# Strided attention heads on four 64x64 quadrants of the PE array

## The chip, the cores and the metric

The kernel runs on one core of a Trainium2 chip, as one launch. Its time is the device time of that launch in microseconds (us); the kernel before took 598.16 us in the median of three runs (596.69 to 599.0). A core has five engines with their own instruction streams: PE (the matrix array; the profile shows its weight loads apart, as PEld), DVE (vector), ACT (scalar), POOL and SP. Here SP issues nearly all input transfers, in order.

## The reference

Two parts follow each other. The first is attention over 8 batches and 8 heads of 576 positions and 64 features, in float32. Heads 0 to 3 see the 32 latest positions (local). Heads 4 to 7 see the positions of the same residue modulo 32 that are not later (strided):

```python
scores = scale * np.matmul(q, k.transpose(0, 1, 3, 2))
mask_local = (rel >= 0) & (rel < stride)
mask_strided = (rel >= 0) & (pos[None, :] % stride == pos[:, None] % stride)
...
attn = np.exp(scores)
attn = attn / (np.sum(attn, axis=-1, keepdims=True) + 1e-09)
return np.matmul(attn, v).astype(np.float32)
```

For a strided head this is 32 separate problems, one for each residue, of 18 queries by 18 keys. The second part is a mixture of experts: each of the 4608 rows of 512 numbers goes to the best of 8 experts (512 to 1024 to 512, relu) and is weighted by its gate.

## The kernel before

The attention is cut into 32 units: 16 local ones (two batches, one head) and 16 strided ones (`Strided`, one batch, two heads), which take turns. The order of PE's instructions is written out by hand in the loop over `n`: scores of unit `n`, transposes (`turn`) of unit `n-2`, masks of unit `n+1`, values of unit `n-3`, and then pieces of the routing of finished batch pairs (`xl`, `lg`, `xs`, `lt`, `rk`, `en` in the rows). The orders on DVE, ACT and POOL come from a scheduler at build time, which places instructions by its own estimates. Transfers on SP are held back behind named PE instructions (`behind`), three units ahead for q and k. PSUM is one pool of eight banks; a bank is used again when its last reader is done. After the attention the expert part runs from some 165 us to the end; the change leaves its code alone.

A strided unit does this. `prep` copies q into a block-diagonal buffer `qz` (L408: one head on DVE, the other on ACT), with zeros between, so that one product over 128 rows gives the scores of both heads for one residue. `masks` writes the causal mask into one PSUM bank by a bf16 product (L412). `scores` adds 32 products of 36 weight columns and 18 moving columns (L419). A float32 product is two instructions with weights of their own, so the trace counts 64. Softmax runs over 288 columns: L431, L433, L436, L437, L438, L440 on DVE, and L434 (exponential) on ACT. `turn` makes four transposes (L218, tile `ts`) and spreads them into `eb`, with zeros between residues: half by DVE (L450), half by ACT (L454, twice). `values` makes 16 products over 72 rows (four residues of 18 keys), 64 weight columns, 72 moving columns (L464), and ACT copies both banks out (L472). In both products the output rows 0 to 63 and 64 to 127 belong to two column halves of the array, and each product uses the array's full height.

Of the kernel before, what the change touches and what calls it, by code (L numbers as in the profile page):

```python
# [11 lines left out]
F32 = mybir.dt.float32  # L12
# [34 lines left out]
BIG = -float(2 ** 30)  # L47
# [4 lines left out]
C_RE8 = C_ID + P  # L52
C_SIO = C_RE8 + E
C_P = C_SIO + NBP * LA
C_T = C_P + 1
C_F = C_T + 4
C_H = C_F + 4
C_N = C_H + 2

# [6 lines left out]
M_ID = 0  # L66
M_L = M_ID + P
M_S = M_L + 9 * 64
M_TRI = M_S + 16 * 18
M_ONE = M_TRI + P  # L70
M_N = M_ONE + P

# [6 lines left out]
def _block(i, bb):  # L79

    return (i + 2 * bb) % 18


def _constants():
# [7 lines left out]
    for t in range(4):  # L92
        cf[18 * t:18 * t + 18, C_T + t] = 1
# [12 lines left out]
    a = np.arange(18)  # L106
    causal = np.where(a[None, :] <= a[:, None], 0, BIG)
    for j in range(2):
        for h in range(2):
            r0 = 64 * j + 18 * h  # L110
            cb[r0:r0 + 18, M_S:M_S + 288] = np.tile(causal, (1, 16))
    cb[:, M_TRI:M_TRI + P] = -(np.arange(P)[:, None] >= np.arange(P)[None, :]).astype(np.float32)
    cb[:, M_ONE:M_ONE + P] = 1
    tok = P * np.arange(36)[None, :] + np.arange(P)[:, None]
    return cf, cb.astype(ml_dtypes.bfloat16), tok.astype(np.float32)


def _layout(q, k, v, moe_modality_id, moe_w_gate, moe_modality_bias, moe_w1, moe_w2):
    q, k, v = (np.asarray(t, np.float32) for t in (q, k, v))
# [7 lines left out]
    vr = v[:, :4].reshape(NBP, 2, 4, 18, 32, D).transpose(0, 2, 1, 3, 4, 5)  # L127
# [3 lines left out]
    for bb in range(2):  # L131
        for i in range(18):
# [3 lines left out]
            w = win[:, :, i % 2, :, 2 * (i // 2) + bb] if i < 16 else win[:, :, i - 16, :, 16 + bb]  # L136
# [11 lines left out]
    vs = v[:, 4:].reshape(B, 2, 2, 18, 4, 2, 4, D).transpose(0, 1, 6, 3, 4, 5, 2, 7)  # L148
    vs = np.ascontiguousarray(vs).reshape(B, 2, 72, 1024)
# [10 lines left out]
    cf, cb, tok = _constants()  # L160
# [22 lines left out]
def attention_moe(ctx: ExitStack, tc: tile.TileContext, a, out):  # L183
    nc = tc.nc
# [6 lines left out]
    def pa(name):  # L191
        return ps.tile([P, 512], F32, tag="a", name=name)
# [38 lines left out]
    pin = tc.keep_in_program_order  # L231
# [8 lines left out]
    def behind(dma, last):  # L240
        return pin(follow(dma, last))
# [45 lines left out]
    qzs = zeros(2, [P, 32, 2, 18], "qz")  # L287
    for t in qds + ets:
        nc.vector.memset(t[:], 0.0)
    for t in qzs:  # L290
        nc.gpsimd.memset(t[:], 0.0)


    class Local:
# [92 lines left out]
    class Strided:  # L387
# [9 lines left out]

        def load_values(self, part, last):
            if part == 0:
                self.vs = lp.tile([72, 8, 2, D], F32, tag="vs", name=f"vs{self.n}")  # L400
                behind(nc.sync.dma_start(self.vs.rearrange("p g h d -> p (g h d)"), a["vs"][self.b, self.pr]), last)
# [8 lines left out]
        def masks(self):  # L410
            self.s = pa(f"ss{self.n}")[:, :288]
            nc.tensor.matmul(self.s, identb, cb[:, M_S:M_S + 288], start=True, stop=True)  # L412

        def scores(self):
            n, qz, s = self.n, self.qz, self.s
            for i in range(16):
                for j in range(2):
                    r = (i // 4) * 8 + j * 4 + i % 4
                    at["scores"] = nc.tensor.matmul(  # L419
                        s[64 * j:64 * j + 36, 18 * i:18 * i + 18],  # L420
                        qz[:, r, :, :].rearrange("p h q -> p (h q)"),
                        self.qk[:, 1, 18 * r:18 * r + 18],
                        start=False, stop=True, skip_group_check=True,
                    )
            s3 = s.rearrange("p (i k) -> p i k", i=16)

            def bc(t):
                return t.unsqueeze(2).to_broadcast([P, 16, 18])

            mx = lp.tile([P, 16], F32, tag="mxs", name=f"mxs{n}")  # L430
            nc.vector.tensor_reduce(mx[:], s3, AX.X, ALU.max)  # L431
            ex = lp.tile([P, 16, 18], F32, tag="exs", name=f"exs{n}")
            nc.vector.tensor_tensor(ex[:], s3, bc(mx), ALU.subtract)  # L433
            nc.scalar.activation(ex[:], ex[:], AF.Exp, scale=0.125)  # L434
            sm = lp.tile([P, 16], F32, tag="sms", name=f"sms{n}")
# [3 lines left out]
            self.en = lp.tile([P, 16, 18], F32, tag="ens", name=f"ens{n}")  # L439
            nc.vector.tensor_tensor(self.en[:], ex[:], bc(sm), ALU.mult)  # L440

        def turn(self):
            n = self.n
            tp = pa(f"ts{n}").rearrange("p (g q) -> p g q", g=4)
            for g in range(4):
                turned_to(tp[0:72, g, :], self.en[:, 4 * g:4 * g + 4, :])
            self.eb = eb = lp.tile([72, 8, 4, 36], F32, tag="eb", name=f"eb{n}")
            src = tp[0:72].rearrange("p g (j x) -> p (g j) x", j=2)[:, :, 0:36]
            sh = [72, 8, 2, 36]
            nc.vector.tensor_tensor(  # L450
                eb[:, :, 0:2, :], src.unsqueeze(2).to_broadcast(sh),
                cf[0:72, C_T:C_T + 2].unsqueeze(1).unsqueeze(3).to_broadcast(sh), ALU.mult)
            for t in (2, 3):
                nc.scalar.activation(eb[:, :, t, :], src, AF.Copy, scale=cf[0:72, C_T + t:C_T + t + 1])  # L454

        def values(self):
            n, eb, vs, b = self.n, self.eb, self.vs, self.b
            for g2 in range(2):
                ot = pa(f"ot{n}{g2}")[:, :288]
                for g in (2 * g2, 2 * g2 + 1):  # L460
                    for j in range(2):
                        c = (g % 2) * 144 + 72 * j
                        for h in range(2):
                            at["values"] = nc.tensor.matmul(  # L464
                                ot[64 * h:64 * h + 64, c:c + 72],
                                vs[:, 2 * g + j, h, :],
                                eb[:, 2 * g + j, :, 18 * h:18 * h + 18],
                                start=True, stop=True, skip_group_check=True,
                            )
                base = (b % 2) * S  # L470
                dst = self.xc[:, base:base + S].rearrange("p (q r) -> p r q", r=32)[:, 16 * g2:16 * g2 + 16, :]
                nc.scalar.copy(dst, ot.rearrange("p (r q) -> p r q", r=16))  # L472

    rows = []

# [515 lines left out]
    for ph, (bp, n) in enumerate(PHASES):  # L991
        last = ph == len(PHASES) - 1
# [154 lines left out]
```

## Time and profile before

| | us |
|---|---|
| median of 3 runs | 598.16 |
| lowest, highest | 596.69, 599.0 |
| the profiled execution, whole | 600.58 |
| its span (first to last instruction) | 598.8 |
| mean granted clock of PE in it | 0.986 of full |

The profiled execution is 2.42 us above the median. Its span lacks 1.78 us that lie around it. Busy times overlap where instructions are pipelined, so a sum of durations is larger than the time that they take; the chain of waits gives the steps without that overlap. A row of the trace is one instruction or several alike (`x64`). `issue` is time in which an engine waits for nothing that the profile shows.

### The profile page before, as it was taken

How to read it: one execution, taken by the hardware profiler on the slowest of the kernel's cores; microseconds unless marked ns; L12 is line 12 of the kernel's file. 1: busy time of each engine (PE TensorE's matmuls, PEld its weight loads, DVE VectorE, ACT ScalarE, POOL GpSimd, SP SyncE). 2: the span in 40 equal slices, each digit the busy share in tenths (PEclk: the TensorE clock that was granted, in tenths of full speed). 3: DMA queues.
4: the chain of work that ended last, by engine and by line, in shares of the span. 5: the costliest groups of instructions: out<-in, count | busy, mean ns of one | idle time of the engine just before them, and what ended most of it. 6: DMA issues, size and time to landing. Idle time of an engine off the chain costs nothing.

```text
span 598.8 us, 15262 instructions
## 1 busy us (share of the span) xinstructions
PE 574.2 (96%) x5995; PEld 508.0 (85%) x5997; DVE 439.1 (73%) x1092; ACT 395.0 (66%) x814; POOL 249.0 (42%) x226
## 2 busy tenths in 40 slices
PE   8998889897999999999999999999999999999995
PEld 5887778776879898999999989999999999999995
DVE  6885967954868799668687687687687787787542
ACT  5897868764785676676566576665665665665652
POOL 1021101126247636554544746546545646532311
PEclk9999989988899999999999999999999999999998
DMA  8997978987745843744843844213214239514631
GB/s 316 301 295 218 346 242 282 318 293 248 253 108 159 235 146 97 235 156 103 243 153 98 221 168 92 71 37 106 71 36 106 71 113 278 110 45 71 221 103 50
DMA packets 72482, 102.03 MB, mean 170 GB/s; under 512 B 48019, under 2 KB 48275, under 8 KB 68820
## 3 DMA queue, kind: packets, MB, share of 16 engines
q0 software_dynamic: 20672, 58.01, 29.1%
q1 hardware_dynamic: 51252, 42.48, 26.7%
q8 instruction: 49, 0.80, 0.6%
q10 hardware_dynamic: 480, 0.51, 0.3%
q14 instruction: 29, 0.24, 0.1%
HBM read 123.45 MB, written 19.18 MB: 238 GB/s over the span
## 4 chain that ended last, share of the span: by engine, by line
PE 85%; DVE 4%; issue 4%; DMA 3%; ACT 2%; POOL 0%; SPq 0%; POOLq 0%; ACTq 0%; DVEq 0%
PE h L921 34%; PE o L935 33%; PE o L369 3%; PE ot L464 2%; DMA vs<-in_vs 2%; PE s L334 2%; PE ss L419 2%; PE xs L218 1%; PE lg L524 1%; PE t L218 1%; PE ts L218 1%; PE xl L218 1%; DMA qks<-in_qks 1%; PE en L620 1%; ACT wh L956 1%
## 5 line engine op out<-in xcount | busy, mean ns | idle before, releaser
L957 DVE TENSOR_TENSOR wl<-raw,wh 128x512 fp32r<-128x512 f32 x288 | 187.8, 692 | 66.0 <-ACT wh L956 52.5
L956 ACT CAST wh<-raw 128x512 fp32r<-128x512 f32 x288 | 163.9, 619 | 71.5 <-PE o L935 49.5
L921 PE MATMUL h<-xh,wl 128*128 128x256 f32 x576 | 162.7, 283 | 0.0
L921 PE MATMUL h<-xl,wh 128*128 128x256 f32 x576 | 162.6, 283 | 0.0
L921 PE MATMUL h<-xh,wh 128*128 128x256 f32 x576 | 162.4, 282 | 0.2 <-ACT wh L956 0.2
L803 POOL DMA_INDIRECT raw<-in_w,wi x72 | 92.6, 1286 | 158.1 <-DVE wl L957 121.4
L921 PEld LDWEIGHTS h<-xh,wh 128*128 128x128 f32 x576 | 109.5, 190 | 7.6 <-issue 0.6
L921 PEld LDWEIGHTS h<-xl,wh 128*128 128x128 f32 x576 | 109.6, 190 | 5.5
L935 PE MATMUL o<-wh,hh 128*128 128x512 f32 x288 | 114.3, 397 | 0.0
L935 PE MATMUL o<-wl,hh 128*128 128x512 f32 x288 | 113.8, 395 | 0.0
L921 PEld LDWEIGHTS h<-xh,wl 128*128 128x128 f32 x576 | 109.7, 190 | 1.0
L935 PE MATMUL o<-wh,hl 128*128 128x512 f32 x288 | 110.3, 390 | 0.0
L924 ACT ACTIVATE hh<-h 128x256 fp32r<-128x256 f32 x144 | 55.4, 384 | 67.2 <-PE h L921 50.1
L926 DVE SCALAR_TENSOR_TENSOR hl<-h,hh 128x256 fp32r<-128x256 f32 x144 | 60.7, 421 | 30.7 <-ACT hh L924 23.4
L935 PEld LDWEIGHTS o<-wh,hl 128*128 128x128 f32 x288 | 53.5, 188 | 11.0
L935 PEld LDWEIGHTS o<-wh,hh 128*128 128x128 f32 x288 | 54.6, 189 | 7.8 <-ACT hh L924 0.2
L935 PEld LDWEIGHTS o<-wl,hh 128*128 128x128 f32 x288 | 54.6, 190 | 5.6
L943 POOL DMA_INDIRECT out<-y,le x36 | 44.2, 1229 | 20.7 <-ACT y L942 11.0
L794 POOL DMA_INDIRECT le<-ld,li x36 | 39.6, 1101 | 12.9 <-issue 10.1
L787 POOL DMA_INDIRECT fx<-xd,le x36 | 40.1, 1115 | 11.0 <-issue 10.7
L479 POOL DMA_DIRECT2D xd<-xt x20 | 14.5, 725 | 61.9 <-ACT xt L488 61.9
L369 PEld LDWEIGHTS o<-vv,et 128*64 128x64 f32 x512 | 21.2, 156 | 10.1 <-issue 7.6
(192 smaller groups left out, 779.8 us busy)
## 6 DMA issues: line engine op xcount, KB each, us to landing
vv<-in_vl SPq DMA_DIRECT2D x32, 292.5 KB
qks<-in_qks SPq DMA_DIRECT2D x32, 288.0 KB
xd<-xt POOLq DMA_DIRECT2D x16, 512.0 KB
qk<-in_qkl SPq DMA_DIRECT2D x16, 304.0 KB
qk<-in_qkl SPq DMA_DIRECT2D x16, 288.0 KB
vs<-in_vs SPq DMA_DIRECT2D x16, 288.0 KB
raw<-in_w,wi POOLq DMA_INDIRECT x72
xd<-xt POOLq DMA_DIRECT2D x4, 256.0 KB
```

Source lines behind the costliest of these rows:

```text
L218: at["turn"] = nc.tensor.transpose(dst, src, ident)
L369: at["values"] = nc.tensor.matmul(o[64 * jj:64 * jj + 64, k, :], et[:, u, :, :].rearrange("p g q -> p (g q)"), vv[:, u, :], start=True, st ...
L787: pin(nc.gpsimd.indirect_dma_start(xt[:, h, :], None, xd[0:xrows, :], IOA(ap=le[:, h, 0:1], axis=0)))
L794: pin(nc.gpsimd.indirect_dma_start(le[:, h, :], None, ld[0:xrows, :], IOA(ap=li[:, s, h:h + 1], axis=0)))
L803: pin(nc.gpsimd.indirect_dma_start(raws[j].rearrange("p f c -> p (f c)"), None, a["w"], IOA(ap=wi[:, s, j:j + 1], axis=0), bounds_check=E ...
L921: nc.tensor.matmul(hp, w[:, a1], x[:, c, :], start=(k == 0), stop=(k == 11))
L924: nc.scalar.activation(hh[:], hp, AF.Relu)
L926: nc.vector.scalar_tensor_tensor(hl[:], hp, 0.0, hh.bitcast(F32), ALU.max, ALU.subtract)
L935: nc.tensor.matmul(os[h], hx[:, m], w[:, 512:1024], start=(f == 0 and i == 0), stop=(f == 7 and i == 2))
L943: outs.add(pin(nc.gpsimd.indirect_dma_start(out, IOA(ap=le[:, h, 0:1], axis=0), y[:], None, bounds_check=NT - 1, oob_is_err=False)))
L956: nc.scalar.copy(wh[:, c], raw[:, c])
L957: nc.vector.tensor_tensor(wl[:, c], raw[:, c], wh[:, c].bitcast(F32), ALU.subtract)
```

## The change

Three residues (54 positions) are taken together, or two (36) where 16 residues of a half leave four over: `_residues` gives 3, 3 and 2 times two groups for each half. Scores are now products of one head: 64 rows (its features), 54 or 36 weight columns, as many moving columns, straight from `qk`; so `prep` does nothing, and `qz` and its zeroing on POOL go. Head `h` lies on rows 64h to 64h+63 of the array and writes a bank of its own, and group `j` lies on columns 64j and up: four quadrants. The 54x54 result holds three wanted 18x18 blocks; the rest is masked (`three`). So there are two banks of 324 columns, and two mask products. A unit has 24 score products in place of 32.

Softmax runs over these wider rows: two maxima and two subtractions of 324 columns, and one exponential, one sum and one multiplication of 648. The masked zeros now stand where `eb` needs them, so `turn` makes six transposes of 128x128 into two banks and ACT copies these plainly (512 and 256 columns). `values` makes 24 products over 54 or 36 rows (keys of three or two residues), 64 weight columns, 54 or 36 moving columns, in quadrants again: key half on rows, head on columns. v comes in four transfers (54x512 twice, 36x256 twice) in place of one of 72x1024, with the same 288 KB of data; the last two wait for the values of the unit before.

```diff
+            c, rn = ((slice(0, 512), 54), (slice(512, 768), 36))[part]
+            for half in range(2):
+                r = slice(64 * half, 64 * half + rn)
+                behind(nc.sync.dma_start(dst[r, c], a["vs"][self.b, self.pr, half, 0:rn, c]), last)
...
         def prep(self):
-            self.qz = qz = qzs[self.n % 2]
-            for h in range(2):
-                r = slice(64 * h, 64 * h + 64)
-                dst, src = qz[r, :, h, :], self.qk[r, 0, :].rearrange("p (r q) -> p r q", q=18)
-                pin(nc.scalar.copy(dst, src) if h else nc.vector.tensor_copy(dst, src))
+            pass
...
+            for sl in range(6):
+                for j in range(2):
+                    r0, nr = _residues(sl % 2, sl // 2, j)
+                    w, c = 18 * nr, slice(18 * r0, 18 * r0 + 18 * nr)
+                    for h in range(2):
+                        r = slice(64 * h, 64 * h + 64)
+                        at["scores"] = nc.tensor.matmul(
+                            self.s[h][64 * j:64 * j + w, 54 * sl:54 * sl + w], qk[r, 0, c], qk[r, 1, c],
...
+                s3, g = self.s[h].rearrange("p (i k) -> p i k", i=6), slice(6 * h, 6 * h + 6)
+                nc.vector.tensor_reduce(mx[:, g], s3, AX.X, ALU.max)
+                nc.vector.tensor_tensor(ex[:, g, :], s3, bc(mx[:, g], 6), ALU.subtract)
...
+            for i0, i1 in ((0, 4), (4, 6)):
+                tp = pa(f"ts{n}{i0}").rearrange("p (g q) -> p g q", g=4)
+                for i in range(i0, i1):
+                    turned_to(tp[:, i - i0, :], self.en[:, 2 * i:2 * i + 2, :])
+                nc.scalar.copy(eb[:, i0:i1, :], tp[:, 0:i1 - i0, :])
...
+                            at["values"] = nc.tensor.matmul(
+                                ot[half][64 * h:64 * h + 64, c:c + w], vs[r, ga, j, h, :],
+                                eb[r, 3 * h + ga, 64 * j:64 * j + w],
```

On PE, one strided unit between its masks and the next transposes stands like this before (`ss` scores, `ot` values, `ts` transposes):

```order
L412 MATMUL ss_767<-cb_sb 128x288
L464 MATMUL ot_769<-eb_683,vs_595 64x72 x8
L464 MATMUL ot_779<-eb_683,vs_595 64x72 x8
L419 MATMUL ss_767<-qks_554,qz_105 36x18 x32
L218 MATMUL ts_837<-cf_sb,ens_675 72x128 x4
```

In the changed kernel the same place has two mask products and the end of the values, of two residues each (the wider ones stand between):

```order
L422 MATMUL ss_769<-cb_sb 128x324
L422 LDWEIGHTS cb_sb
L422 MATMUL ss_770<-cb_sb 128x324
L473 MATMUL ot_773<-eb_679,vs_590 64x54 x2
L473 MATMUL ot_774<-eb_679,vs_590 64x54 x2
...
L473 MATMUL ot_773<-eb_679,vs_590 64x36 x2
L473 MATMUL ot_774<-eb_679,vs_590 64x36 x2
```

Values alternate between the two key halves and their two banks; nothing moved across another stage.

On DVE, between the subtraction of a strided unit (`exs`) and the sum of its exponentials (`sms`), which waits for ACT, stand before eight instructions of the local unit (`rs`, `xt`, `mx`) and the copy for the next scores:

```order
L433 TENSOR_TENSOR exs_827<-ss_767,mxs_825 128x288
L380 TENSOR_SCALAR rs_863<-o_852 128x5
L381 RECIPROCAL rs_863<-rs_863 128x5
L382 TENSOR_TENSOR xt_116<-o_852,rs_863 128x5x64
L380 TENSOR_SCALAR rs_876<-o_867 128x4
L381 RECIPROCAL rs_876<-rs_876 128x4
L341 TENSOR_REDUCE mx_885<-s_848 128x4
L382 TENSOR_TENSOR xt_116<-o_867,rs_876 128x4x64
L408 COPY qz_106<-qks_724 64x32x18
L436 TENSOR_REDUCE sms_830<-exs_827 128x16
```

In the changed kernel the sum of the same unit comes at once:

```order
L444 TENSOR_REDUCE mxs_831<-ss_769 128x6
L444 TENSOR_REDUCE mxs_831<-ss_770 128x6
L445 TENSOR_TENSOR exs_832<-ss_769,mxs_831 128x324
L445 TENSOR_TENSOR exs_832<-ss_770,mxs_831 128x324
L448 TENSOR_REDUCE sms_838<-exs_832 128x12
L389 TENSOR_SCALAR rs_872<-o_861 128x5
```

This is so in two of the 16 strided units; in the others three to ten instructions of other work stand between.

## Rows read from the trace of the kernel before

**Rows 1.** The page's head.

```profile
span 598.8 us, 15262 instructions
```

**Rows 2.** Busy time by stretch: stretch, length, PE, PEld, DVE, ACT, POOL, clock, DMA, GB/s.

```profile
0.00:165.00 165.00, 147.38 (x3234) 123.28 (x3237) 122.58 (x456) 121.91 (x274) 31.97 (x45) 0.96 0.87 283
165.00:598.80 433.80, 426.86 (x2763) 384.74 (x2761) 316.47 (x637) 273.12 (x541) 217.00 (x181) 1.00 0.45 127
22.00:30.00 8.00, 7.54 (x212) 6.68 (x212) 7.03 (x22) 7.58 (x17) 0.00 (x0) 1.00 0.95 284
30.00:38.00 8.00, 6.88 (x209) 6.22 (x207) 7.38 (x23) 7.04 (x16) 3.00 (x6) 1.00 0.98 291
62.00:70.00 8.00, 6.91 (x201) 6.12 (x199) 7.87 (x35) 6.82 (x16) 1.06 (x1) 1.00 1.03 330
110.00:118.00 8.00, 7.09 (x198) 6.48 (x195) 7.90 (x37) 6.00 (x14) 2.04 (x4) 1.00 0.99 346
```

**Rows 3.** Chain of waits, PE pieces: start, length, engine, tile, line, count.

```profile
70.62 1.00 PE en L620 x18
...
73.94 2.42 issue
...
107.99 1.05 PE s L334 x35
...
112.19 1.23 PE ss L419 x64
113.42 0.56 PE ts L218 x4
...
118.47 1.15 PE ot L464 x32
...
128.86 1.86 PE lg L524 x32
...
134.30 0.12 PE ss L412
```

**Rows 4.** Chain of waits, DVE pieces.

```profile
58.68 0.66 DVE eb L450
59.34 0.37 DVE exs L433
...
61.89 0.36 DVE qz L408
...
63.08 0.40 DVE mx L341
```

**Rows 5.** Groups by line and shape, 0 to 170 us: count, busy us, mean ns, idle before.

```profile
L454 ACT ACTIVATE eb<-ts,cf_sb 72x288 f32<-72x288 f32 x32 | 14.1, 490 | 7.8 <-DVE eb L450 7.5
...
L408 ACT COPY qz<-qks 64x576 f32<-64x576 f32 x16 | 10.8, 673 | 2.1 <-DMA qks<-in_qks 1.7
...
L495 ACT COPY xc<-xl 128x512 f32<-128x512 f32 x16 | 9.0, 594 | 1.0 <-PE xl L218 0.9
...
L341 DVE TENSOR_REDUCE mx<-s 128x5 f32<-128x320 f32 x16 | 7.6, 477 | 1.1 <-remote 1.1
...
L434 ACT ACTIVATE exs<-exs 128x288 f32<-128x288 f32 x16 | 7.1, 443 | 0.4
...
L341 DVE TENSOR_REDUCE mx<-s 128x4 f32<-128x256 f32 x16 | 6.6, 413 | 8.0 <-PE s L334 6.4 <-PE t L218 1.6
...
L344 ACT ACTIVATE ex<-ex 128x128 f32<-128x128 f32 x16 | 4.7, 295 | 0.0
```

**Rows 6.** Timeline: start, length, engine, line, operation, idle before it and its releaser.

```profile
7.06 0.45 DVE L408 COPY qz<-qks 64x576 f32<-64x576 f32 x1 [1.91 <-DMA qks<-in_qks]
...
33.05 1.22 PE L464 MATMUL ot<-eb,vs 72*64 72x72 f32 x32 [0.67 <-DMA vs<-in_vs]
...
35.83 0.60 PE L218 MATMUL ts<-cf_sb,ens 128*72 128x128 f32 x4 [0.45 <-DVE ens L440]
```

**Rows 7.** DMA issues of v: count, KB each.

```profile
vs<-in_vs SPq DMA_DIRECT2D x16, 288.0 KB
```

More of the change, by code (lines that the diff above doesn't have):

```diff
@@ L54 @@
 C_P = C_SIO + NBP * LA
-C_T = C_P + 1
-C_F = C_T + 4
+C_F = C_P + 1
 C_H = C_F + 4
@@ L81, in _block, with _residues @@
     return (i + 2 * bb) % 18
+def _residues(half, a, j):
+    return (16 * half + 6 * a + 3 * j, 3) if a < 2 else (16 * half + 12 + 2 * j, 2)
 def _constants():
@@ L91, in _constants @@
     cf[:, C_F:C_F + 4] = P * np.arange(4)
-    for t in range(4):
-        cf[18 * t:18 * t + 18, C_T + t] = 1
     cb = np.zeros((P, M_N), np.float32)
@@ L107, in _constants @@
     causal = np.where(a[None, :] <= a[:, None], 0, BIG)
+    three = np.full((54, 54), BIG, np.float32)
+    for t in range(3):
+        three[18 * t:18 * t + 18, 18 * t:18 * t + 18] = causal
     for j in range(2):
-        for h in range(2):
-            r0 = 64 * j + 18 * h
-            cb[r0:r0 + 18, M_S:M_S + 288] = np.tile(causal, (1, 16))
+        cb[64 * j:64 * j + 54, M_S:M_S + 324] = np.tile(three, (1, 6))
     cb[:, M_TRI:M_TRI + P] = -(np.arange(P)[:, None] >= np.arange(P)[None, :]).astype(np.float32)
@@ L146, in strided_t @@
         return np.ascontiguousarray(t).reshape(B, 2, P, S)
-    vs = v[:, 4:].reshape(B, 2, 2, 18, 4, 2, 4, D).transpose(0, 1, 6, 3, 4, 5, 2, 7)
-    vs = np.ascontiguousarray(vs).reshape(B, 2, 72, 1024)
+    vr = v[:, 4:].reshape(B, 2, 2, 18, 32, D).transpose(0, 1, 4, 3, 2, 5)
+    vs = np.zeros((B, 2, 2, 54, 3, 2, 2, D), np.float32)
+    for half in range(2):
+        for ga in range(3):
+            for j in range(2):
+                r0, nr = _residues(half, ga, j)
+                vs[:, :, half, :18 * nr, ga, j] = vr[:, :, r0:r0 + nr].reshape(B, 2, 18 * nr, 2, D)
+    vs = vs.reshape(B, 2, 2, 54, 768)
     w1 = np.asarray(moe_w1).reshape(E, 4, P, 8, P).transpose(0, 3, 2, 1, 4).reshape(E, 8, P, 512)
@@ L286, in attention_moe @@
     ets = zeros(1, [P, 18, 2, 32], "et")
-    qzs = zeros(2, [P, 32, 2, 18], "qz")
+    ens = zeros(2, [P, 12, 64], "en")
     for t in qds + ets:
         nc.vector.memset(t[:], 0.0)
-    for t in qzs:
-        nc.gpsimd.memset(t[:], 0.0)
+    for t in ens:
+        nc.gpsimd.memset(t[:, :, 54:], 0.0)
     class Local:
@@ L410, in masks @@
[L410 to L433, printed above, removed]
+                self.vs = lp.tile([P, 3, 2, 2, D], F32, tag="vs", name=f"vs{self.n}")
@@ new lines, in load_values, with masks @@
+            c, rn = ((slice(0, 512), 54), (slice(512, 768), 36))[part]
+            dst = self.vs.rearrange("p a j h d -> p (a j h d)")
+            for half in range(2):
+                r = slice(64 * half, 64 * half + rn)
+                behind(nc.sync.dma_start(dst[r, c], a["vs"][self.b, self.pr, half, 0:rn, c]), last)
+        def prep(self):
+            pass
+        def masks(self):
+            self.s = [pa(f"ss{self.n}{h}")[:, :324] for h in range(2)]
+            for s in self.s:
+                nc.tensor.matmul(s, identb, cb[:, M_S:M_S + 324], start=True, stop=True)
@@ new lines, in scores, with bc @@
+        def scores(self):
+            n, qk = self.n, self.qk
+            for sl in range(6):
+                for j in range(2):
+                    r0, nr = _residues(sl % 2, sl // 2, j)
[4 more added lines that the diff above has]
+                            self.s[h][64 * j:64 * j + w, 54 * sl:54 * sl + w], qk[r, 0, c], qk[r, 1, c],
+                            start=False, stop=True, skip_group_check=True,
+                        )
+            mx = lp.tile([P, 12], F32, tag="mxs", name=f"mxs{n}")
+            ex = lp.tile([P, 12, 54], F32, tag="exs", name=f"exs{n}")
+            def bc(t, k):
+                return t.unsqueeze(2).to_broadcast([P, k, 54])
+            for h in range(2):
+                s3, g = self.s[h].rearrange("p (i k) -> p i k", i=6), slice(6 * h, 6 * h + 6)
+                nc.vector.tensor_reduce(mx[:, g], s3, AX.X, ALU.max)
+                nc.vector.tensor_tensor(ex[:, g, :], s3, bc(mx[:, g], 6), ALU.subtract)
@@ L438, in scores @@
             nc.vector.reciprocal(sm[:], sm[:])
-            self.en = lp.tile([P, 16, 18], F32, tag="ens", name=f"ens{n}")
-            nc.vector.tensor_tensor(self.en[:], ex[:], bc(sm), ALU.mult)
+            self.en = ens[n % 2]
+            nc.vector.tensor_tensor(self.en[:, :, 0:54], ex[:], bc(sm, 12), ALU.mult)
         def turn(self):
             n = self.n
-            tp = pa(f"ts{n}").rearrange("p (g q) -> p g q", g=4)
-            for g in range(4):
-                turned_to(tp[0:72, g, :], self.en[:, 4 * g:4 * g + 4, :])
@@ L447, in turn @@
[L447 to L454, printed above, removed]
+            self.eb = eb = lp.tile([P, 6, P], F32, tag="eb", name=f"eb{n}")
@@ L456, in values @@
+            for i0, i1 in ((0, 4), (4, 6)):
[3 more added lines that the diff above has]
+                nc.scalar.copy(eb[:, i0:i1, :], tp[:, 0:i1 - i0, :])
         def values(self):
             n, eb, vs, b = self.n, self.eb, self.vs, self.b
[L458 to L462, printed above, removed]
+            ot = [pa(f"ot{n}{half}")[:, :288] for half in range(2)]
@@ L463, in values @@
+            for ga in range(3):
+                for j in range(2):
+                    for half in range(2):
+                        r0, nr = _residues(half, ga, j)
+                        w, c = 18 * nr, 18 * (r0 - 16 * half)
+                        r = slice(64 * half, 64 * half + w)
                         for h in range(2):
                             at["values"] = nc.tensor.matmul(
-                                ot[64 * h:64 * h + 64, c:c + 72],
-                                vs[:, 2 * g + j, h, :],
@@ L472, in values @@
-                nc.scalar.copy(dst, ot.rearrange("p (r q) -> p r q", r=16))
+                dst = self.xc[:, base:base + S].rearrange("p (q r) -> p r q", r=32)[:, 16 * half:16 * half + 16, :]
+                nc.scalar.copy(dst, ot[half].rearrange("p (r q) -> p r q", q=18))
     rows = []
```

9 lines of the change are left out of this document (3 added, 6 removed).

## The prediction

> **What bounds the kernel now.** I read the busy time by stretch first. The reader is to see two parts: the expert part, 165 us to the end, where PE is busy 426.86 of 433.80 us, and the attention before it, where PE is busy 147.38 of 165 us, DVE 122.58, ACT 121.91 and the DMA engines 0.87 of the time [rows 2]. The change touches the attention alone, so I leave the 433.80 us as they are; all that follows is about some 160 us, 27% of the span of 598.8 [rows 1].
>
> In the attention no engine is full all the time. The stretches show the difference: at 22 to 38 us DVE is busy 7.03 and 7.38 of 8 us, ACT 7.58 and 7.04 and DMA 0.95 and 0.98, and PE is the one that waits (0.45 us for DVE's `ens`, 0.67 us for v) [rows 2, 6]. At 62 to 70 and 110 to 118 us DVE is busy 7.87 and 7.90 of 8 [rows 2]. These four stretches are 32 us and hold about five of the 16 strided units. In the rest the chain of waits runs through PE, piece after piece, broken by `issue` (2.42 us at 73.94) [rows 3]. So I count PE's change in 11 units and DVE's in 5.
>
> **PE, scores and values.** Before, 64 score records take 1.23 us (19.2 ns each) and 32 value records 1.15 us (36 ns each); together 2.38 us [rows 3]. After, a unit has 24 score and 24 value products, two records each: 96 records, 64 of them with 54 moving columns and 32 with 36. What a record costs in a quadrant is not in the trace, since every product before spans the full height. The nearest rows are those on column strips. `en` uses one strip alone: 18 records of 64 columns in 1.00 us, 56 ns each, or 0.87 ns a column. `s` uses two strips: 35 records of the same 64 columns in 1.05 us, 30 ns, half of that. `lg` uses four strips with 256 columns: 0.87 x 256 = 223 ns on one strip, and 32 records in 1.86 us are 58 ns each, so 3.8 of four ran side by side [rows 3]. If two column halves and two row halves do the same, a record costs 0.87 x 54 / 4 = 11.7 ns, or 7.8 with 36 columns: 64 x 11.7 + 32 x 7.8 = 1.00 us. If only the column halves overlap, it is 23.4 ns, and for 36 columns the 19.2 that `ss` shows as the shortest: 64 x 23.4 + 32 x 19.2 = 2.11 us. If nothing overlaps, 64 x 47 + 32 x 31 = 4.0 us; I give this little weight, as strips overlap in every row that uses them. If quadrants overlap but no record comes faster than 19.2 ns, 96 x 19.2 = 1.84 us. Between 1.00 and 2.11 I take the middle, 1.5 us: the overlap of strips speaks for the low end, the 19.2 ns of 18 columns (which alone would be 8 on two strips) for a floor.
>
> The `ss` row shows that floor: 64 records at 19.2 ns [rows 3]. The Trainium skill, "TensorEngine Tiling (Array Packing)", section Instruction Overhead, says that each matmul carries some 60 cycles, so that one column costs as much as 60, and that no tiling factor should be taken from a dimension that is small already. By it the 54 and 36 columns would each cost 25 ns at 2.4 GHz, an estimate from that page: 96 x 25 = 2.4 us, and nothing would be won. The trace goes below it, with 19.2 ns.
>
> **PE, masks and transposes.** One mask product of 288 columns takes 0.12 us; two of 324 take 2 x 0.135 = 0.27. Four transposes take 0.56 us, 0.14 each, six take 0.84 [rows 3]. Both stand in PE's order, nothing hides them: +0.15 and +0.28 us. So a unit goes from 1.23 + 1.15 + 0.56 + 0.12 = 3.06 us to 1.5 + 0.27 + 0.84 = 2.61: -0.45 us. The ends are -0.95 (1.00 us of products), +0.16 (2.11) and +2.05 (4.0). In 11 units: -5.0 us, ends -10.5 and +1.8, far end +22.5.
>
> **DVE.** Removed: `qz` 0.36 us and `eb` 0.66. Changed: four steps of 288 columns at 0.37 become four of 324 and two of 648 (the sum and the multiplication) [rows 4]. A column costs (477 - 413) / 64 = 1.0 ns [rows 5], which agrees with 0.40 us for a step of 320 [rows 4]; so 324 columns are 0.41 and 648 are 0.73. 4 x 0.41 + 2 x 0.73 = 3.10 against 4 x 0.37 + 0.36 + 0.66 = 2.50: +0.60 us a unit. In the five units of the full stretches that is +3.0 us; in the other eleven it stays in DVE's idle time (122.58 of 165 us are busy; 11 x 0.6 more are 129 [rows 2]). The exponential of 648 columns goes from 443 to 443 + 360 x (443 - 295) / 160 = 776 ns [rows 5], and where the sum stands right behind the subtraction, as in two units, DVE stops for it: 2 x 0.8 = 1.6 at most. Behind that sum are queued `rs` and `xt`, which free the banks of the local values; PE comes to these banks an iteration later, so I count a third, +0.5. In the other units instructions stand between. DVE: +3.5 us, ends 0 and +1.6 + 16 x 0.6 = 11.2.
>
> **ACT.** `qz` goes (673 ns), the exponential grows by 333, and 2 x 490 for `eb` become a copy of 512 columns, 594, and one of 256, at most the 490 of 288 [rows 5]: -0.67 + 0.33 + 0.10 = -0.24 us a unit, or -3.8 in 16. Where ACT is full DVE is as well [rows 2], so I count nothing; ends 0 and -1.5 (six units).
>
> **Transfers and the start.** v stays at 288 KB a unit [rows 7], in four transfers. Three more issues by SP lie beside its waits for PE. The last two pieces are released after the values in place of the transposes; SP's next entry, q or k three units ahead, waits for the same PE instruction, so nothing is queued behind them that was free before. Where DMA is full (22 to 38 us [rows 2]) they stand behind older data anyway. I count 0; ends -1 and +2 (three more waits of 0.67 [rows 6]). At the start DVE stands 1.91 us for q and k of the first strided unit and copies 0.45 [rows 6]; with the copy gone this wait moves to PE, where the products need the same data, and I count the copy alone, -0.5 us.
>
> PSUM: a unit holds six of the eight banks' turns where it held four, so PE's transposes now reuse a score bank one stage earlier. Between the score products and that point lie the transposes, a local unit's values and its scores, about 3 us, against 4 x 0.41 on DVE; I count nothing unless DVE is late, which is the third rival.
>
> **The sum.** -5.0 + 3.5 - 0.5 = -2.0 us. Against the profiled execution's own time, 600.58 us, that is 598.6; it lay 2.4 us above the median of the runs shown, so against 598.16 I forecast 596.2 us.
>
> **The rivals.**
> First, quadrants fully side by side, and DVE's longer steps hidden: products 1.00 us, 11 x -0.95 - 0.5 = -11 us, 587. For it: `lg` overlaps 3.8 of 4. Against: 19.2 ns in `ss`, and DVE at 7.9 of 8.
> Second, the row halves do not run side by side, so that the quadrants give no more than the strips: 11 x 0.16 + 3.5 - 0.5 = +4.8 us, 603. For it: no row shows two heights at once. It decides as soon as a record costs over 20 ns.
> Third, on the other side too, DVE becomes the bound throughout: +0.6 us in each of 16 units and 1.6 us for the two bare exponentials, less 0.5: +10.7, 609. It decides where DVE has no idle time to take 0.6 us in a unit, and PE then waits for `en` before its transposes. For it: the 0.45 us wait for `ens` [rows 6]. Against: 42 us of idle DVE in 165 [rows 2].
> Fourth, by the rule on the 60 cycles, 25 ns a record gives PE +0.45 us a unit, the same sign as the second rival with 11 x 0.45 + 3 = +8, 606; I count it within the second.
>
> **How the numbers follow.** Chances: forecast 0.45 (592 to 601), first rival 0.18, second with the fourth 0.22, third 0.15. A measurement of this kernel tells about 0.5% from no change, 3 us: faster is below 595.2, slower above 601.1. Of the forecast's 0.45 I put 0.18 below 595.2 and 0.27 between; the first rival is all faster, the second 0.07 within and 0.15 above, the third 0.01 and 0.14. That makes faster 0.36, same 0.35, slower 0.29. The range runs from 587 to 607: it leaves out the outer half of the first and third rivals.
>
> **What would show it.** Right: 96 `ss` and `ot` records of a unit in 1.3 to 1.7 us; six transposes in 0.84; DVE 0.6 us more a unit, with its stretches at 22 to 38, 62 to 70 and 110 to 118 us still the full ones; `qz` gone from ACT; an attention that ends some 2 us earlier and an expert part of the same length. Wrong: records above 20 ns; PE waiting over 0.5 us for `en` in most units, or for a PSUM bank behind `exs`; PE waiting longer for v; more `issue` time where PE's records come faster.

## The result and the profile after

| | before | changed |
|---|---|---|
| median of 10 runs each, us | 598.33 | 605.15 |
| lowest, highest | 593.21, 602.36 | 601.52, 608.14 |
| ratio, 95% interval | | 1.0136 [1.010, 1.0172] |

The changed kernel is slower by 1.36%, about 8 us; forecast was 2 us faster. Its profiled execution took 602.88 us with a span of 601.0, in the faster half of its runs, while the profiled execution before was at the slow end of its own. So the two traces differ by less than the medians.

The page's head and the busy time by stretch of the changed kernel, the stretches of [rows 2]:

```profile
span 601.0 us, 15389 instructions
```

```profile
0.00:165.00 165.00, 142.88 (x3266) 116.27 (x3267) 128.91 (x449) 113.84 (x254) 31.05 (x45) 0.94 0.85 278
165.00:601.00 436.00, 429.11 (x2781) 386.82 (x2779) 318.10 (x645) 277.77 (x546) 206.56 (x181) 1.00 0.46 129
22.00:30.00 8.00, 6.58 (x189) 5.80 (x190) 7.03 (x22) 6.97 (x15) 0.00 (x0) 1.00 0.95 297
30.00:38.00 8.00, 5.56 (x167) 4.60 (x168) 5.85 (x18) 5.21 (x12) 3.17 (x6) 1.00 0.79 261
62.00:70.00 8.00, 6.58 (x184) 5.72 (x184) 7.52 (x33) 6.44 (x16) 0.73 (x1) 0.94 0.97 340
110.00:118.00 8.00, 7.96 (x152) 6.93 (x153) 7.50 (x28) 4.87 (x12) 2.61 (x4) 0.79 0.81 241
```

PE is busy 4.5 us less in the first 165 us (142.88 against 147.38), DVE 6.3 us more, and none of the four stretches is fuller on DVE than before.

PE's busy time hides a second difference, in the column of the granted clock: 0.96 before [rows 2] and 0.94 after, and 0.79 at 110 to 118 us, where PE is busy 7.96 us with only 152 records. In both traces the clock is granted either in full (2.4 GHz) or at half (1.2 GHz), so these means stand for some 13 and 20 us of the 165 at half clock. At one clock PE's busy time would differ by some 8 us in place of 4.5 (an estimate from these rows). Not all of that is the quadrants': the attention ends later after the change, so less of the work behind it falls into the stretch. Each of the six falls of the changed trace came just behind a stop of PE of 0.8 to 1.9 us; four of these stops are the stall in the values that is told below. No run here shows that the stop brings the fall.

The attention nevertheless ends later. Its last values stand in the timeline at 160.67 before and at 163.43 after (the row of 139.59 is one that nothing stops):

```profile
160.67 1.22 PE L464 MATMUL ot<-eb,vs 72*64 72x72 f32 x32
```

```profile
139.59 0.91 PE L473 MATMUL ot<-eb,vs 54*64 54x54 f32 x48
...
163.43 0.96 PE L473 MATMUL ot<-eb,vs 54*64 54x54 f32 x48
```

The sizes of the steps, first in the chain of waits of the changed kernel [rows 3], then by line and shape over 0 to 170 us [rows 5]:

```profile
64.55 0.74 DVE sms L448
...
68.02 0.78 DVE en L452
```

```profile
115.64 0.28 PE ss L422 x2
...
118.37 0.69 PE ss L432 x48
119.05 0.81 PE ts L227 x6
```

```profile
L444 DVE TENSOR_REDUCE mxs<-ss 128x6 f32<-128x324 f32 x32 | 14.3, 484 | 7.2 <-PE ss L432 7.2
L445 DVE TENSOR_TENSOR exs<-ss,mxs 128x324 f32<-128x324 f32 x32 | 14.2, 482 | 0.0
L452 DVE TENSOR_TENSOR en<-exs,sms 128x648 f32<-128x648 f32 x16 | 13.3, 829 | 0.2
L448 DVE TENSOR_REDUCE sms<-exs 128x12 f32<-128x648 f32 x16 | 13.1, 821 | 3.3 <-ACT exs L446 3.2
L446 ACT ACTIVATE exs<-exs 128x648 f32<-128x648 f32 x16 | 11.9, 746 | 6.3 <-DVE exs L445 6.1
```

The quadrants do work side by side: 48 score records take 0.69 us, 14.4 ns each, against 19.2 [rows 3].

What is new is a stall in the values. PE and DVE in the timeline of one round of the changed kernel:

```profile
65.13 0.44 PE L422 MATMUL ss<-cb_sb 128*128 128x324 bf16 x2
65.50 0.32 PE L473 MATMUL ot<-eb,vs 54*64 54x54 f32 x4
66.73 0.89 PE L473 MATMUL ot<-eb,vs 54*64 54x54 f32 x44 [0.91 <-issue]
```

```profile
63.99 0.48 DVE L391 TENSOR_TENSOR xt<-o,rs 128x320 f32<-128x320 f32 x1
64.39 0.16 DVE L598 TENSOR_TENSOR new<-cum,ohb 128x8 bf16<-128x8 bf16 x1
64.47 0.82 DVE L448 TENSOR_REDUCE sms<-exs 128x12 f32<-128x648 f32 x1
...
66.21 0.41 DVE L391 TENSOR_TENSOR xt<-o,rs 128x256 f32<-128x256 f32 x1
```

The values write two banks, and PE stops at the first product of the second. By the timing this was a bank of local values `o`, whose last reader is the second `xt`. On DVE the sum `sms` now stands ahead of that `xt`; `xt` ends at 66.62 and PE goes on at 66.73. The profile calls the gap `issue`; the end of `xt` 0.1 us earlier names it. The trace has six such stops between 5 and 165 us, 4.9 us together. Four of them (3.1 us) end 0.1 us after an `xt`. The other two (1.8 us) end 0.1 us after the local subtraction `ex`, which reads a bank of local scores; it too stands behind the sum:

```profile
36.37 0.83 PE L473 MATMUL ot<-eb,vs 54*64 54x54 f32 x42 [1.29 <-issue]
```

```profile
32.36 0.83 DVE L448 TENSOR_REDUCE sms<-exs 128x12 f32<-128x648 f32 x1 [1.50 <-ACT exs L446]
...
34.25 0.82 DVE L452 TENSOR_TENSOR en<-exs,sms 128x648 f32<-128x648 f32 x1
...
35.85 0.41 DVE L351 TENSOR_TENSOR ex<-s,mx 128x256 f32<-128x256 f32 x1
```

Summed over 0 to 170 us, the idle time ahead of values and transposes stands behind the last bar of these rows, before and after:

```profile
L464 PE MATMUL ot<-eb,vs 72*64 72x72 f32 x512 | 20.7, 228 | 2.9 <-issue 1.7 <-DMA vs<-in_vs 0.9
L218 PE MATMUL ts<-cf_sb,ens 128*72 128x128 f32 x64 | 10.8, 295 | 2.7 <-DVE ens L440 1.4 <-DVE pos L585 1.3
```

```profile
L227 PE MATMUL ts<-cf_sb,en 128*128 128x128 f32 x96 | 17.3, 327 | 4.1 <-DVE en L452 3.5 <-DVE sml L583 0.5
L473 PE MATMUL ot<-eb,vs 54*64 54x54 f32 x512 | 13.7, 227 | 5.9 <-issue 4.9 <-ACT et L365 0.9
L473 PE MATMUL ot<-eb,vs 36*64 36x36 f32 x256 | 7.6, 219 | 1.2 <-DMA vs<-in_vs 1.2
```

That is 5.6 us before and 11.2 after. In the order of DVE's instructions the sum stands ahead of one or both `xt` of its round in 13 of 16 units; before, in 3.

### The profile page after: what moved, and what is told of

Read it like the earlier page. It is cut to its first block, busy times and chain, and to the rows that moved or that the text cites. A ratio compares the mean times of both kernels' runs of the same rounds, so it can differ in the third digit from the quotient of the medians.

```text
span 601.0 us, 15389 instructions
## 1 busy us (share of the span) xinstructions
PE 572.0 (95%) x6045; PEld 503.1 (84%) x6045; DVE 447.0 (74%) x1092; ACT 391.6 (65%) x798; POOL 237.6 (40%) x226
## 4 chain that ended last, share of the span: by engine, by line
PE 83%; ACT 5%; DVE 4%; issue 3%; DMA 3%; POOL 0%; SPq 0%; POOLq 0%; ACTq 0%
PE h L930 34%; PE o L944 33%; PE o L378 3%; PE s L343 2%; DMA vs<-in_vs 2%; PE ts L227 2%; PE ot L473 1%; PE lg L533 1%; PE t L227 1%; PE xs L227 1%; ACT et L365 1%; ACT xc L481 1%; DMA qk<-in_qkl 1%; ACT qd L326 1%; DVE ex L351 1%
## 5 line engine op out<-in xcount | busy, mean ns | idle before, releaser
L812 POOL DMA_INDIRECT raw<-in_w,wi x72 | 83.4, 1159 | 174.5 <-DVE wl L966 131.0
L803 POOL DMA_INDIRECT le<-ld,li x36 | 39.4, 1094 | 12.9 <-issue 10.4
L365 ACT COPY et<-t 64x512 f32<-64x512 f32 x32 | 18.5, 578 | 21.0 <-PE t L227 20.6
```

Source lines behind the costliest of these rows:

```text
L365: nc.scalar.copy(et[r, 0:16, par, :], t1[r].rearrange("p k (u q) -> p (k u) q", u=4))
L803: pin(nc.gpsimd.indirect_dma_start(le[:, h, :], None, ld[0:xrows, :], IOA(ap=li[:, s, h:h + 1], axis=0)))
L812: pin(nc.gpsimd.indirect_dma_start(raws[j].rearrange("p f c -> p (f c)"), None, a["w"], IOA(ap=wi[:, s, j:j + 1], axis=0), bounds_check=E ...
```

## The experiments

Each is given as a ratio to the kernel before, which ran again on the same chip beside it, with its 95% interval. The runs lie on several chips, so two ratios of different runs are compared only through the kernel before.

### Banks, amount of work

`b_7banks`: the kernel before with one PSUM bank less.

```diff
-    ps = ctx.enter_context(tc.tile_pool(name="ps", bufs=8, space=bass.MemoryType.PSUM))
+    ps = ctx.enter_context(tc.tile_pool(name="ps", bufs=7, space=bass.MemoryType.PSUM))
```

> The kernel before with a PSUM pool of seven banks in place of eight, nothing else. Bank theory (the changed kernel loses because a strided unit takes six bank turns in place of four, so that PE waits for readers): a unit pair then has 10 turns on 7 banks, 1.43 a bank, near the changed kernel's 12 on 8, 1.5 (before: 1.25): +4 to +8 us on 598, with PE idle before the products of `ot`, `s`, `o` until DVE or ACT has read a bank. DVE theory (it loses because DVE has 0.6 us more to do in each strided unit): 0 to +1 us.

1.0014 [0.9965, 1.0064]. Fewer banks alone cost nothing that can be told, to half a per cent.

`b_sums_twice`: the kernel before with more DVE work in a unit.

```diff
-            nc.vector.tensor_reduce(sm[:], ex[:], AX.X, ALU.add)
+            for _ in range(2):
+                nc.vector.tensor_reduce(sm[:], ex[:], AX.X, ALU.add)
...
-            nc.vector.tensor_tensor(self.en[:], ex[:], bc(sm), ALU.mult)
+            for _ in range(2):
+                nc.vector.tensor_tensor(self.en[:], ex[:], bc(sm), ALU.mult)
```

> The kernel before, with the sum and the multiplication of each strided unit made twice: 2 x 0.37 = 0.74 us more of DVE a unit, a little over the changed kernel's 0.60; banks, PE, ACT and transfers as they were. DVE theory: +5 to +9 us. Bank theory: 0 to +2 us, as DVE is idle for 42 of the first 165 us.

1.0111 [1.0073, 1.0149]. I first took this for the amount of work. But the scheduler had also moved the sums: they stood ahead of one or both `xt` in 8 of 16 units, where it was 3. Its mean granted clock was lower too (0.977, the kernel before beside it 0.984). It doesn't tell these apart.

`a_5turns`: the changed kernel, all six transposes into one bank.

```diff
+            tp = pa(f"ts{n}").rearrange("p (g q) -> p g q", g=4)
+            for i in (4, 5, 0, 1, 2, 3):
+                turned_to(tp[:, i % 4, :], self.en[:, 2 * i:2 * i + 2, :])
             for i0, i1 in ((0, 4), (4, 6)):
-                tp = pa(f"ts{n}{i0}").rearrange("p (g q) -> p g q", g=4)
-                for i in range(i0, i1):
-                    turned_to(tp[:, i - i0, :], self.en[:, 2 * i:2 * i + 2, :])
```

> The changed kernel, where the last two of the six transposes of a unit go first and into the bank of the other four, which then overwrite them; ACT copies the 256 columns from there. Same instructions on every engine, one bank turn less in a unit (five in place of six); the attention weights of two of six column groups are those of others. Bank theory: 2.5 to 5 of the 8 us come back, 600 to 603, and PE's waits of 1 us before `ot`, `s` and `o` shrink. DVE theory: 605 to 606 as before.

1.0112 [1.0071, 1.0153]. The theory of the banks falls as a cause of its own.

`a_short_sums`: the changed kernel, sum and multiplication over 288 columns.

```diff
-            nc.vector.tensor_reduce(sm[:], ex[:], AX.X, ALU.add)
+            nc.vector.tensor_reduce(sm[:], ex[:, :, 0:24], AX.X, ALU.add)
...
+                self.en[:, :, 0:24], ex[:, :, 0:24], sm.unsqueeze(2).to_broadcast([P, 12, 24]), ALU.mult)
```

> The changed kernel with the sum and the multiplication over 288 of their 648 columns; the other columns are left out and read as zeros. DVE has 2 x 0.36 = 0.72 us less a unit, so it is back at the kernel before; banks, PE, ACT, transfers as in the changed kernel. DVE theory: 6 to 8 us come back, 597 to 599. Bank theory: 1 to 3 us come back (DVE frees banks sooner), 602 to 604.

1.0021 [0.9979, 1.0062]. Nearly all comes back. This fits less work, and just as well a shorter instruction ahead of `xt` and ahead of `en`. The place did not change: the sum still stands ahead of one or both `xt` in 13 of 16 units. So an early place costs by the length of what stands there.

### Place or amount

`a_order`: the sums behind both `xt`, no work less. The sum, its small steps and the multiplication become a method `weigh`, called after the values.

```diff
+            follow(nc.vector.tensor_reduce(sm[:], ex[:], AX.X, ALU.add), at["xt"])
...
+        if n < nu and isinstance(units[n], Strided):
+            units[n].weigh()
```

> The changed kernel with one thing moved: on DVE the sum, the reciprocal and the multiplication of a strided unit now stand behind both `xt` of the local unit of the same iteration, no longer ahead of one of them. Amount of DVE work and PE's order are as in the changed kernel. Theory A (DVE is late, by amount and by place: `sms` stops for the exponential and holds up the `xt` that frees a bank of local values): the waits of `ot` of about 1 us go, those of `ts` for `en` get longer; ratio to the kernel before 1.004 to 1.010. Theory A without the place (only the amount counts): 1.011 to 1.016, as the changed kernel. Rival B (smaller pieces of v arrive late): no change, 1.011 to 1.016, so it doesn't tell B from the latter.

1.0035 [1.0002, 1.0068]: three quarters of the loss (1.0136) went with the place.

`a_nomax`: the changed kernel, no maximum, no subtraction.

```diff
-                nc.vector.tensor_reduce(mx[:, g], s3, AX.X, ALU.max)
-                nc.vector.tensor_tensor(ex[:, g, :], s3, bc(mx[:, g], 6), ALU.subtract)
-            nc.scalar.activation(ex[:], ex[:], AF.Exp, scale=0.125)
+                nc.scalar.activation(ex[:, g, :], s3, AF.Exp, scale=0.125)
```

> The changed kernel, in which ACT takes the exponential of the strided scores straight from the two score banks (two activations of 324 columns), with no maximum and no subtraction on DVE; the softmax is the same without them as long as nothing overflows. DVE has four steps of 324 columns less, 4 x 0.41 = 1.64 us a unit, which is 1.04 less than the kernel before; ACT frees the score banks. Theory A (DVE's lateness is the loss, and the quadrants save PE about 0.7 us of products and give back 0.43 in masks and transposes): ratio to the kernel before 0.985 to 0.995, and not slower than `b_nomax` by more than 0.3%. Rival B (transfers of v): 1.008 to 1.014. Rival C (the quadrants don't pay on PE even where DVE is free): above `b_nomax` by over 0.5%.

1.0143 [1.0086, 1.0199]. Theory A was wrong here: with less DVE work than before the change the loss is all there. Rivals B and C allow this ratio too; `a_v2` and `a_nomax_late` take them up. The groups of its trace over 0 to 170 us:

```profile
L470 PE MATMUL ot<-eb,vs 54*64 54x54 f32 x512 | 14.9, 230 | 12.8 <-issue 11.8 <-ACT et L365 0.9
L445 DVE TENSOR_REDUCE sms<-exs 128x12 f32<-128x648 f32 x16 | 13.2, 827 | 34.2 <-ACT exs L443 34.2
```

DVE reaches the sum earlier, stands 34.2 us for ACT's exponential, and the readers of the local banks wait behind it, so PE's wait for the banks of its values more than doubles (11.8 us under `issue` against 4.9). More of these stops end 0.1 us after the local subtraction `ex` (7.5 us) than after an `xt` (4.3 us).

`b_nomax`: the same edit in the kernel before, on its score bank.

> The kernel before with the same edit: ACT takes the exponential of the strided scores straight from the score bank, no maximum and no subtraction; DVE has two steps of 288 columns less, 0.74 us a unit. Theory A: DVE's time counts before the change too, so 0.986 to 0.997. If DVE's time counts only where it is over what the kernel before has: 0.997 to 1.003. Rival B says nothing of it beyond 1.00.

1.0018 [0.9978, 1.0057]: nothing is won there either.

`a_v2`: v in two transfers at the transposes.

```diff
-            c, rn = ((slice(0, 512), 54), (slice(512, 768), 36))[part]
...
-                behind(nc.sync.dma_start(dst[r, c], a["vs"][self.b, self.pr, half, 0:rn, c]), last)
+                    r = slice(64 * half, 64 * half + 54)
+                    behind(nc.sync.dma_start(dst[r, :], a["vs"][self.b, self.pr, half]), last)
```

> The changed kernel with v in two transfers of 54x768 (one for each key half), both released at the transposes, in place of four, of which two wait for the values; 18 rows of the last 256 columns are moved though nobody reads them, so 324 KB in place of 288. Theory A: the waits for v were 2.6 us in four places and most stay or move, ratio to the kernel before 1.010 to 1.017. Rival B (the late pieces of v are the loss): 1.006 or less.

1.0116 [1.0058, 1.0174]. The late pieces of v are not the loss, or little of it: the interval reaches down to 1.0058.

### The same question in the kernel before, and where the wait went

`a_nomax_late`: `a_nomax` with the sums behind both `xt` (the edits of `a_order` and `a_nomax` together).

> `a_nomax` (exponential straight from the score banks, 1.64 us less DVE work a unit than the changed kernel) with the sums held behind both `xt`, as in `a_order`. There DVE stood 34 us at `sms`. Theory P: these stops go, ratio to the kernel before 0.988 to 0.999, under `a_order`. If the loss of `a_nomax` is something else (ACT's exponential in the way of its copies, or the score banks freed later): above 1.008.

1.0020 [0.9987, 1.0052]; theory P gave 0.988 to 0.999, which the interval just reaches. With `a_order` this makes a square: sums early 1.0136 with maximum and 1.0143 without, sums late 1.0035 and 1.0020. The place is worth 1.0 to 1.2%, the 1.64 us of maximum and subtraction in a unit nothing that can be told. A part of the place's price goes through the clock: `a_nomax` had a mean granted clock of 0.983 over its runs, the kernel before beside it 0.991; for `a_nomax_late` it is 0.985 and 0.984. Here the timeline of DVE shows what the late place costs instead:

```profile
21.49 0.83 DVE L453 TENSOR_TENSOR en<-exs,sms 128x648 f32<-128x648 f32 x1
25.71 0.17 DVE L389 TENSOR_SCALAR rs<-o 128x5 f32<-128x5 f32 x1 [3.38 <-PE o L384]
```

DVE idles 3.38 us until PE has the local values, while the next sum, whose exponential is done by 24.6, stands behind their `xt`; PE then waits for `en`. The transposes of `a_order` show the same wait, the values hardly one:

```profile
L227 PE MATMUL ts<-cf_sb,en 128*128 128x128 f32 x96 | 14.6, 290 | 9.5 <-DVE en L456 6.2 <-ACT xc L485 1.5 <-DVE po L596 1.1
...
L477 PE MATMUL ot<-eb,vs 54*64 54x54 f32 x512 | 11.8, 224 | 0.7 <-ACT et L365 0.7
```

`b_early`: the kernel before with the second `rs` and `xt` behind the sum.

```diff
+                rs1 = nc.vector.tensor_scalar(rs[:, :gn], o[:, :, D], 1e-9, None, ALU.add)
+                if bb == 1:
+                    follow(rs1, at["sums"])
```

> The kernel before with only the place changed: on DVE the second `rs` and `xt` of the local unit stand behind the sum `sms` of the strided unit of the same iteration, as in the changed kernel; no DVE work is added. Theory P (place: `sms` stops for the exponential, `xt` behind it frees the bank of local values late, and PE waits): ratio 1.004 to 1.012, with waits of `ot` for a bank; the sum is 0.4 us shorter than in the changed kernel, so less than its 1.0136. Theory M (only the amount of DVE work counts): 0.997 to 1.003.

1.0102 [1.0057, 1.0147], as theory P expected, but not by its wait: the values wait 0.5 us in all and the scores 15.3.

```profile
L421 PE MATMUL ss<-qks,qz 128*36 128x18 f32 x1024 | 26.3, 199 | 15.3 <-ACT xc L474 6.2 <-issue 5.0 <-ACT ex L344 3.4
L466 PE MATMUL ot<-eb,vs 72*64 72x72 f32 x480 | 18.8, 229 | 0.5 <-issue 0.5
```

The copy `qz`, which the scores need, had fallen behind that `xt` on DVE; PE goes on 0.1 us after its end (70.94), and the `ACT xc` that the profile names copies values, which the scores do not read:

```profile
70.17 0.41 DVE L384 TENSOR_TENSOR xt<-o,rs 128x256 f32<-128x256 f32 x1
70.50 0.44 DVE L410 COPY qz<-qks 64x576 f32<-64x576 f32 x1
```

```profile
71.05 2.11 PE L421 MATMUL ss<-qks,qz 128*36 128x18 f32 x64 [2.38 <-ACT xc L474]
```

So the agreement with theory P is luck: the run shows that a later place of one small DVE step costs 1%, not that this one does. And of this 1% (6.2 us) most can be the clock: its mean over the runs was 0.975 here and 0.984 in the kernel before beside it, which on 604 us is some 5.5 us of PE at full clock (an estimate from these means).

`b_twice_late`: `b_sums_twice` with the sums held behind both `xt`. `b_nomax_late`: `b_nomax` with the same.

> The kernel before with the sum and the multiplication done twice (0.74 us more DVE work a unit, as in `b_sums_twice`), but with the sums held behind both `xt` of the local unit, so that the place is that of the kernel before. Theory P: most of the 1.0111 of `b_sums_twice` goes, 0.999 to 1.005. Theory M: 1.008 to 1.014, as there.

> `b_nomax` with the sums held behind both `xt`: the same edits in the kernel before, for the comparison of the quadrants alone once DVE neither stops nor is full. Theory P: 0.990 to 0.999. If the quadrants pay on PE as the trace's durations say (0.3 us a unit of products, masks and transposes together, 5 us in 16): `a_nomax_late` lies 0.3 to 0.9% under it; if they don't pay even then: no lower.

1.0358 [1.0309, 1.0406] and 1.0119 [1.0062, 1.0176]. No theory on record gives either. Again `qz` is late, and the clock is lower (0.964 and 0.974, against 0.984). In `b_nomax_late` 8 of the 14 us that the scores wait end 0.1 us after `qz`; in `b_twice_late` it ran at 76.99, behind both sums and both multiplications, and PE's scores stood for it:

```profile
77.54 1.69 PE L419 MATMUL ss<-qks,qz 128*36 128x18 f32 x54 [3.39 <-ACT qd L317]
```

The profile names ACT's last instruction here, which had long been done; `qz` on DVE ended at 77.4. These two say nothing of the quadrants.

### An order in which nothing is late

`a_prompt`: `a_order`, and the local maximum behind `en`. So each round on DVE is: both `xt`, sum, reciprocal, `en`, then the local softmax.

```diff
+            at["en"] = nc.vector.tensor_tensor(self.en[:, :, 0:54], ex[:], bc(sm, 12), ALU.mult)
...
-                nc.vector.tensor_reduce(m, s, AX.X, ALU.max)
+                follow(nc.vector.tensor_reduce(m, s, AX.X, ALU.max), at["en"])
```

> The changed kernel with DVE's order in each round set to: both `xt` of the local unit, then sum, reciprocal and multiplication of the strided unit, then the local maximum. No work is added or left out. Theory P (the loss is the order: `xt` late or `en` late): neither `ot` nor `ts` waits for DVE over 0.5 us in most units, ratio to the kernel before 0.990 to 1.000. Rival G (PE has no gain to give back, since something else sets the rounds, or DVE's round is simply full): 1.002 or more, with the wait moved on to the next user of a local score bank or to `t`.

1.0011 [0.9976, 1.0045], between what theory P and what rival G gave. The loss is gone, with all the work of the changed kernel done. The waits of `ts` and `ot`:

```profile
L227 PE MATMUL ts<-cf_sb,en 128*128 128x128 f32 x96 | 14.5, 289 | 2.8 <-DVE en L456 1.7 <-DVE ex L351 0.6 <-ACT xc L485 0.2
L477 PE MATMUL ot<-eb,vs 54*64 54x54 f32 x512 | 13.3, 224 | 3.2 <-issue 3.1
```

`b_prompt`: the same order in the kernel before, by the same two lines.

> The kernel before with the same order on DVE (both `xt`, then sum, reciprocal, multiplication, then the copy `qz` and the local maximum). Theory P: the kernel before had hardly any of these waits, so 0.996 to 1.003, above `a_prompt` by 0.3 to 0.9%, which is what the quadrants are worth. Rival G: at or under `a_prompt`.

1.0013 [0.9973, 1.0054]. The order is worth nothing to the kernel before, which was not late, and with it the quadrants are worth nothing either, as rival G had it; both statements hold to about half a per cent. In the stretch of 0 to 160 us PE is busy 6.4 us less in `a_prompt` (first) than in `b_prompt`:

```profile
0.00:160.00 160.00, 139.93 (x3284) 111.98 (x3288) 136.06 (x464) 114.66 (x258) 30.63 (x45) 0.99 0.87 290
```

```profile
0.00:160.00 160.00, 146.38 (x3240) 122.11 (x3241) 127.71 (x456) 122.31 (x275) 31.68 (x45) 0.97 0.89 292
```

Some 3 of these 6.4 us are the clock's, granted at 0.99 against 0.97 (0.02 of 160 us, an estimate), so in this pair the quadrants' own share is some 3 us. PE's waits in 5 to 165 us, summed from the timelines, are 17.7 us in `a_prompt` and 12.9 in `b_prompt`: 4.8 us more, which takes that share back. Those that `b_prompt` hardly has are `ot` under `issue` (3.1 us, of which 1.7 end 0.1 us after an `xt`), `s` for a bank that ACT's `xt` holds (2.3) and `ts` for `en` (1.7).

`a_nomax_prompt`: the same order without maximum and subtraction. `a_nomax_split`: the sum free to stand ahead of `xt`, only `en` behind.

> The same order with the exponential taken straight from the score banks (no maximum, no subtraction for the strided scores), so 1.64 us less DVE work a unit. Theory P: 0.985 to 0.998, at or under `a_prompt`. Rival G with DVE full: clearly under `a_prompt`, by over 0.5%. Rival G with something else: as `a_prompt`, above 1.002.

> As `a_nomax_prompt`, but with the sum free to stand ahead of both `xt` and only the multiplication held behind them. In `a_nomax` DVE stood 34 us at the sum, part of it in time that it would have idled. If the stop at the sum itself delays `xt`: above `a_nomax_prompt` by 0.5% or more. If only what follows the sum did (0.4 us of small steps and 0.83 of `en`): within 0.3% of it.

1.0029 [0.9989, 1.0069] and 1.0121 [1.0087, 1.0155]. The first: less DVE work gives nothing even then. The second differs from it in the place of the sum alone, on the same chip: the stop at the sum, with its two small steps and both `xt` behind it, costs nearly all of it again. Its mean granted clock, 0.991, is no lower than that of the kernel before beside it, so this loss is not the clock's. Its row in `a_nomax_split`:

```profile
L449 DVE TENSOR_REDUCE sms<-exs 128x12 f32<-128x648 f32 x16 | 13.2, 827 | 32.6 <-ACT exs L443 32.6
```

`a_prompt_5turns`: the edit of `a_5turns` in `a_prompt`.

> `a_prompt` with the six transposes of a unit into one bank (five turns of the eight banks a unit in place of six), as in `a_5turns`; columns 0 to 255 of the bank are written twice, so part of the values is computed from other heads' weights; the work is the same. If the bank turns eat the gain of the quadrants: 0.992 to 0.998. If they do not (the rounds are set by something else): 0.999 to 1.004, as `a_prompt`.

1.0034 [0.999, 1.0078]. One turn of a bank less does not free the gain of the quadrants. What takes it stays open: several small waits share it, and none of these runs removes them all. No version here beats the kernel before by more than can be told.

## Why the prediction was wrong

**PE, right.** Scores 0.69 us [rows 3 have 1.23]. The values' row in the timeline is 0.91 us where nothing stops them (139.59); the timeline's 1.22 of before is 1.15 in the chain [rows 3, 6], so 0.84: 1.53 us together against 1.5 forecast. Masks 0.28 against 0.27, transposes 0.81 against 0.84. The Trainium skill's rule of some 60 cycles for each matmul ("TensorEngine Tiling (Array Packing)", Instruction Overhead) would give 25 ns a record at 2.4 GHz, an estimate from that page; the trace disagrees with 14.4.

**DVE's sizes, right.** A step of 324 columns takes 484 ns in the groups, one of 648 takes 821 to 829, and the chain has 0.74 for the sum and 0.78 for `en`, where 0.73 was forecast. ACT's exponential was forecast at 776 ns and takes 746.

**The step that failed** is the one on what is queued behind the sum: "PE comes to these banks an iteration later, so I count a third, +0.5. In the other units instructions stand between." The order showed the sum ahead of `xt`, and I looked at two units in which it follows the subtraction at once. What mattered was not how many instructions stand between subtraction and sum, but whether the readers of the local banks, `xt` above all, are among them. The sum stood ahead of one or both `xt` in 3 units before and in 13 after. And PE comes to the bank in the same round: 0.9 us of stall at 66 us, not an iteration later. `a_prompt` puts the size on it: 1.0136 to 1.0011 is 1.25%, some 7.5 us, in place of +0.5. That 605 us still lies between 587 and 607 is luck: no end of that range was drawn for this step.

**The banks.** "I count nothing unless DVE is late" held in its condition: a bank less costs nothing (`b_7banks`), a late reader does.

**PE's gain** was counted at 5.0 us in 11 units. `a_prompt` and `b_prompt` differ by 0.02%, with about half a per cent on either side, so at most some 3 us; of the 6.4 us of busy time some 3 are the clock's, and 4.8 us more of waits stand against the rest. The choice of 11 units in which the chain runs through PE was too many.

**The third rival** had the sign and the size (+10.7 us) and not the mechanism. It said that DVE becomes the bound by its amount of work. Taking 1.64 us a unit off changes nothing at either place of the sums, so the +3.0 us that the sum has for DVE's longer steps is not seen as an amount. Length counts where a reader of a bank waits behind it (`a_short_sums`). DVE was late in its order, with idle time left: 36 us of 165 after the change.

**Transfers**, counted at 0, were that or little more (`a_v2`).

**The clock** has no term in the sum. It was 0.96 and 0.94 in the two traces, some 3 us of PE's work in 165 (0.02 of them, an estimate). In `a_nomax_split` the loss stands without it; how large its part is in the 605.15 us is open.

## What to carry to other kernels

On an engine that runs in order, look at what another engine waits for and at what now stands ahead of it, in every unit and not in two; an engine with idle time can still be the one that is late. Here the place of one instruction of 0.8 us, ahead of the readers of banks, cost nearly four times what the whole change was forecast to give. When an edit changes durations that a scheduler plans by, hold the order fixed first (here: readers of banks, then what the next product needs, then the rest), and only then judge the edit. And read the granted clock beside every busy time: two stretches at 0.99 and 0.97 differ by 3 us in 160 before anything else does.

## What was not expected of the hardware

Records in four quadrants came at 14.4 ns (48 of 54 and 36 columns in 0.69 us), below the 19.2 ns of 18 columns on two halves that I had taken for a floor. And the waits on a bank stood here under `issue`, as did other stops of PE, of 0.8 to 2.9 us, for which I found no engine that ends (2.42 us [rows 3]); only the other engine's timeline tells them apart. Most of the latter share a mark in the traces of both kernels: counted in PE's instructions they stand at one place modulo 256, and a transfer of 16 KB on the queue of instruction transfers begins 2 to 3 us before PE goes on (at 73.8 for the stop that ends at 76.36 in the kernel before). That the transfer is the cause is not shown.
